# An attention block written out by hand: read-outs one per break, output products spread over more head pairs, row maxima turned in a score bank and sent by SyncE

## The chip, the cores and the metric

One core of a Trainium2 chip. The metric is the device time of one execution in microseconds; a kernel's time is the median of several executions. A profile is of one further execution, with its own time.

## The reference

A transformer block with adaptive layer norm: six modulation rows come from a condition vector, attention and a GELU feed-forward follow, each behind a normalization and in front of a gated residual. The attention is causal within four segments of 512 rows and reads a memory of the earlier segments:

```python
x = A_x                                   # 1 x 2048 x 512, 32 heads of 16
h = _layernorm(x) * (1 + ca) + sa
q, k, v = h @ wq, h @ wk, h @ wv          # split in 4 segments of L = 512
for s in range(4):
    logits = einsum("bhqd,bhkd->bhqk", qs, ks) * 16 ** -0.5 + mask
    a_dot = einsum("bhqk,bhkd->bhqd", softmax(logits), vs)
    pq = phi(qs)
    a_mem = (pq @ M) / (pq @ z + 1e-6)
    o = g * a_mem + (1 - g) * a_dot
    M, z = M + phi(ks).T @ vs, z + phi(ks).sum()
x = x + ga * (concat(o) @ wo)
h = _layernorm(x) * (1 + cb) + sb
x = x + gb * (gelu(h @ w1 + b1) @ w2 + b2)
```

## The kernel before, in words

The program is one stream per engine, in an order written out by hand. It has three parts: projections and memory (to about 195 us), attention (to about 620 us), and the feed-forward (to the end). The change lies in the second.

**Head pairs and quads.** The attention part runs over 64 head pairs P; two pairs make a quad Q (32 of them, 8 in each segment), two quads a unit U. The scores of a pair are made twice. `s_part` (L607) makes q times k in parts S0, S1, S2 for the pair P + 4, adds the causal mask by small bf16 products (L628), and VectorE takes the row maxima with `tensor_reduce` (L632). `st_part` (L681) makes k times q, already turned, in parts T0, T1, T2 for the pair P; the negated maxima ride along as three more rows of `qst` (51 rows in L672, 48 in L616), so that ScalarE's exponential (L691) can be taken at once. GpSimd zeroes what lies above the diagonal (L676).

**The maxima's way.** Once both pairs of a quad have their maxima, `m_rows` (L642, GpSimd) splits them into three bf16 terms; `m_put` (L649) turns them on TensorE with a product by an identity (L650) in the PSUM bank `mm`, ScalarE copies the result to `ms` (L124), and two DMAs (L654), issued by ScalarE, write it into rows 48 to 51 and 112 to 115 of the quad's `qst`.

**Read-out.** `pv_part` (L698) multiplies the exponentials of key block j (0 to 3) with V into the bank `pv`, for four heads side by side; block j covers columns 128j to 512. `pv_out` copies the bank to `ts` on ScalarE, and SyncE stores it (L717). Later `pv_in` loads it back with the denominators (L722, L724), `den` makes reciprocals and stores them (L744), `rb_in` loads them broadcast (L750), `mix` applies them, and `o_hi` and `o_lo` split the result.

**Output products.** For each segment but the last, and for each of its four row blocks b, four `wo_part` of three matmuls (L783) sum over the units into the bank `mm`, then `wo_out` adds the residual and SyncE stores it (L802). From these rows the second normalization takes its loads, statistics, applications and transposes (`ln2_*`; `ln2_turn`, L573, in bank `mm` for the first segment).

**The order.** `ORDER` writes out one head pair: `S0 T0 S1 c0 c1 c2 c3 c4 T1 S2 c5 c6 c7 c8 c9 T2`. Between the score parts are two breaks, c0 to c4 and c5 to c9. Everything else is placed by `ap(pos, ...)`: pair pos // 10, place pos % 10. The table `PRM` holds the places: `pv` and `pvout` relative to 20 Q, `mput` and `mrows` likewise, `wo` relative to a row block's start. All score parts of both kinds take the three PSUM score banks `att` in rotation (`bank("att")`), so a part can start only when the exponential or maximum of the part three before has left its bank. There is one bank `pv` and one `mm`; `own` checks that no two users of one overlap.

**SyncE** issues nearly all DMAs of this part in program order: the stores of the read-outs, the stacks `kst` and `qst` of a later quad (L174), the loads of `pv_in`, the reciprocals and the rows for the output products. An issue that waits for its data holds up all behind it.

## Time and profile before

| | us |
|---|---|
| median of 3 runs | 923.02 |
| lowest, highest | 919.65, 923.94 |
| profiled execution, its own time | 920.79 |
| span in its profile | 918.9 |
| first and last store of a read-out | 219.8, 606.1 |

Rows of the timeline show a start, a duration, engine, line, operation, tiles (out <- in), shape, how many instructions are merged, and in brackets the idle time before and what ended it. Rows of the windows view show the stretch, its length, then busy time (and instructions) of PE (TensorE matmuls), PEld (weight loads), DVE (VectorE), ACT (ScalarE) and POOL (GpSimd), then the granted TensorE clock as a share of full speed, the busy share of the DMA engines, and GB/s. Rows of the chain show a start, a length and what the chain passed through. Rows of the waits show the total, the number and the longest. ACTq and SPq are the sequencers of ScalarE and SyncE, where DMAs are issued.

### The profile page before, as it was taken

How to read it: one execution, taken by the hardware profiler on the slowest of the kernel's cores; microseconds unless marked ns; L12 is line 12 of the kernel's file. 1: busy time of each engine (PE TensorE's matmuls, PEld its weight loads, DVE VectorE, ACT ScalarE, POOL GpSimd, SP SyncE). 2: the span in 40 equal slices, each digit the busy share in tenths (PEclk: the TensorE clock that was granted, in tenths of full speed). 3: DMA queues.
4: the chain of work that ended last, by engine and by line, in shares of the span. 5: the costliest groups of instructions: out<-in, count | busy, mean ns of one | idle time of the engine just before them, and what ended most of it. 6: DMA issues, size and time to landing. Idle time of an engine off the chain costs nothing.

```text
span 918.9 us, 14721 instructions
## 1 busy us (share of the span) xinstructions
PE 849.3 (92%) x5289; PEld 577.5 (63%) x5289; DVE 537.2 (58%) x836; ACT 436.5 (48%) x688; POOL 299.5 (33%) x527
## 2 busy tenths in 40 slices
PE   9999999998888889888898889989999999999998
PEld 4877868664444445444444444457788888888887
DVE  7757674565555554555444555677666886553333
ACT  4454444235554554344344554637674533664221
POOL 2213434013564443434574453842310031330000
PEclk9999999997876997865797988989999999999999
DMA  8859464923445574654553465445756563545443
GB/s 324 282 207 348 168 223 151 355 69 95 130 126 121 133 176 114 156 138 112 137 146 105 129 174 156 141 125 197 234 191 235 179 222 111 170 151 179 154 139 114
DMA packets 97137, 156.53 MB, mean 170 GB/s; under 512 B 15396, under 2 KB 31652, under 8 KB 97064
## 3 DMA queue, kind: packets, MB, share of 16 engines
q1 hardware_dynamic: 94472, 153.24, 54.0%
q10 hardware_dynamic: 2592, 2.36, 0.8%
q8 instruction: 41, 0.67, 0.3%
q14 instruction: 32, 0.26, 0.1%
HBM read 93.95 MB, written 60.83 MB: 168 GB/s over the span
## 4 chain that ended last, share of the span: by engine, by line
PE 78%; ACT 6%; DMA 5%; ACTq 4%; DVE 3%; issue 3%; SPq 0%; POOL 0%; DVEq 0%
PE pv L706 11%; PE bx L1024 7%; PE att L672 6%; PE att L616 5%; PE mm L783 5%; PE bx L1289 5%; PE q L317 4%; PE by L1289 4%; PE bv L1289 4%; PE k L317 4%; ACTq L654 4%; ACT pt L691 4%; PE v L468 4%; PE bv L1024 3%; PE att L628 3%
## 5 line engine op out<-in xcount | busy, mean ns | idle before, releaser
L632 DVE TENSOR_REDUCE nm<-att 128x2 f32<-128x1024 f32 (+3 forms) x256 | 201.5, 821 | 184.5 <-PE att L628 160.9
L691 ACT ACTIVATE pt<-att 128x1024 f32<-128x1024 f32 (+1 forms) x192 | 166.2, 882 | 181.5 <-PE att L672 160.6
L676 POOL TENSOR_SCALAR_AFFINE_SELECT pt<-pt 128x256 f32<-128x256 f32 x256 | 103.4, 420 | 198.0 <-ACT pt L691 195.1
L616 PE MATMUL att<-kst,qst 48*128 48x512 f32 (+3 forms) x512 | 96.5, 405 | 52.3 <-ACT pt L691 47.6
L706 PE MATMUL pv<-pt,V 128*32 128x512 f32 (+2 forms) x992 | 108.9, 549 | 0.0
L672 PE MATMUL att<-qst,kst 51*128 51x512 f32 (+3 forms) x512 | 100.1, 421 | 4.8 <-DVE nm L632 4.0
L616 PEld LDWEIGHTS att<-kst,qst 48*128 48x128 f32 x512 | 55.8, 221 | 77.6 <-ACT pt L691 69.0
L672 PEld LDWEIGHTS att<-qst,kst 51*128 51x128 f32 x512 | 51.8, 213 | 56.3 <-DVE nm L632 29.8
L628 PE MATMUL att<-hmask,hid 64*128 64x128 bf16 (+1 forms) x768 | 74.9, 270 | 0.0
L820 POOL TENSOR_TENSOR wb<-wa 128x256 f32<-128x256 f32 x24 | 20.6, 858 | 153.3 <-DMA wa<-in_w 147.8
L706 PEld LDWEIGHTS pv<-pt,V 128*32 128x32 f32 x992 | 26.8, 125 | 37.5 <-issue 33.7
L133 DVE TENSOR_TENSOR gl<-s,gh 128x512 fp32r<-128x512 f32 x34 | 24.4, 718 | 40.9 <-ACT gh L130 40.8
L130 ACT ACTIVATE gh<-s 128x512 fp32r<-128x512 f32 x34 | 21.3, 629 | 46.5 <-PE spare L1289 18.6
L1029 ACT ACTIVATE s<-s,b1t 128x512 f32<-128x512 f32 x42 | 30.2, 720 | 17.9 <-DVE s L1033 17.8
L628 PEld LDWEIGHTS <-hid 64*128 64x128 bf16 x768 | 27.4, 108 | 17.4 <-issue 8.3
L1033 DVE TENSOR_TENSOR s<-bv,s 128x512 f32<-128x512 f32 x28 | 19.2, 686 | 24.4 <-PE bv L1024 19.2
L503 POOL TENSOR_SCALAR qp<-qp 128x512 f32<-128x512 f32 x12 | 18.5, 1539 | 40.7 <-ACT qp L498 40.7
L783 PE MATMUL mm<-woh,oh 128*128 128x512 f32 x52 | 26.9, 517 | 0.0
L317 PE MATMUL q<-Ahh,wqh 128*128 128x512 f32 x64 | 25.9, 404 | 0.0
L133 DVE TENSOR_TENSOR w1ml<-s,w1mh 128x512 fp32r<-128x512 f32 x18 | 13.0, 720 | 21.8 <-ACT w1mh L130 21.8
L317 PE MATMUL q<-Ahl,wqh 128*128 128x512 f32 x64 | 25.6, 400 | 0.0
L317 PE MATMUL k<-Ahh,wkh 128*128 128x512 f32 x64 | 25.4, 398 | 0.0
(355 smaller groups left out, 1942.3 us busy)
## 6 DMA issues: line engine op xcount, KB each, us to landing
GD<-s SPq DMA_DIRECT2D x56, 256.0 KB
s<-GD SPq DMA_DIRECT2D x52, 256.0 KB
kst<-KD SPq DMA_DIRECT2D x64, 192.0 KB
qst<-QD SPq DMA_DIRECT2D x64, 192.0 KB
QD<-q SPq DMA_DIRECT2D x16, 512.0 KB
KD<-k SPq DMA_DIRECT2D x16, 512.0 KB
TD<-ts SPq DMA_DIRECT2D x32, 256.0 KB
xt<-X2D SPq DMA_DIRECT2D x28, 256.0 KB
```

The source lines that it names most:

```text
L133: lo_eng.tensor_tensor(out=lo, in0=src, in1=hi.bitcast(F32), op=ALU.subtract)
L317: pe.matmul(ps, a[:, k, 128 * g:128 * g + 128], b[k], start=(k == 0 and i == 0), stop=(k == KB - 1 and i == 2))
L616: pe.matmul(ps[:, h, lo:lo + n], q_of(P, h, i), k_of(P, h, n), start=c == 0, stop=False, skip_group_check=True)
L628: pe.matmul(dst, hid[r, a], m, start=False, stop=a == 1, skip_group_check=True)
L632: v.tensor_reduce(out=nms[Q][:, 0:8:4, 4 * p + i], in_=ps[:, :, lo:lo + n], axis=AX.X, op=ALU.max, negate=True)
L672: pe.matmul(ps, k[r, P % 2, 128 * j:128 * j + 128], q[r, P % 2, 128 * j:512], start=True, stop=True, skip_group_check=True)
L676: pool.affine_select(out=t, in_=t, pattern=pattern, compare_op=ALU.is_ge, fill=0.0, base=0, channel_multiplier=-1)
L691: act.activation(pt, ps[:, :, :w], AF.Exp, scale=0.25)
L706: pe.matmul(ps[32 * c:32 * c + 32, lo:hi], V[4 * s + j][:, VW * hd:VW * hd + 32], pt[:, c // 2, lo - o:hi - o], start=start, stop=stop)
L783: pe.matmul(ps, a[:, 128 * b:128 * b + 128], w[:, g, :], start=(g == 0 and i == 0), stop=(g == 3 and i == 2))
L1024: pe.matmul(ps, a[:, i, k, :], b[k], start=start and k == 0 and c == 0, stop=k == 1 and c == 2, skip_group_check=not start)
L1289: pe.matmul(ps, a[:, c], w[:, lo:hi], start=(f == 0 and i == 0), stop=(last and i == 2))
```

## The change

Read-out parts: all quads now have key block 0 at c0 and block 1 at c5 of the even pair (the second pair after the quad's own first), block 2 at c0 and block 3 at c5 of the odd pair, one to each break. Before, block 0 stood in the even pair and the other three in the odd one, with two of them (three in the first segment) in one break.

Maxima: the turn is no longer placed by a table and no longer uses `mm`. It is one more product at the end of the score part S2 of an even pair, into columns 256 to 384 of that part's bank (for the last quad a bank of its own), with S2's own scores in columns 0 to 256. SyncE issues the two DMAs. In the first segment the turn stood at c1 of the odd pair before, in the others at c8 of the even pair; now it stands ahead of c5 of the even pair.

Output products: with `mm` free of the turns, the sixteen groups of the first two segments are placed singly, at most two to a pair, in the second half of the first break (c2) or in the second (c6), over ten pairs; those of the third over eight pairs, at c2 and c6. Before, each row block had two groups in one pair and two together at c0 of the next. The buffers of the split results go from five to six.

Second normalization: the first segment's statistics, applications and transposes move to later places; its transposes are done in two steps of two blocks in the score banks, in place of four single ones in `mm`.

```diff
- 'pv': [[[25, 0, 0, 512], [32, 1, 128, 512], [31, 2, 256, 512], [34, 3, 384, 512]],
- ...
+ 'pv': [[[20, 0, 0, 512], [25, 1, 128, 512], [30, 2, 256, 512], [35, 3, 384, 512]]] * 4,
- 'mput': [-9, -12, -12, -12],
- 'wo': [[2, 6, 10, 10], [2, 6, 10, 10], [2, 6, 10, 10]],
- 'woout': [10, 11, 11],
+ 'wo': [[2, 6, 16, 22, 26, 36, 42, 46, 56, 62, 66, 76, 82, 86, 102, 106]] * 2 + [[20 * b + i for b in range(4) for i in (2, 6, 12, 16)]],
- 'ht': [463, 481, 501, 521],
- 'ht1': 644,
- 'ln': [[312, 339, 374, 408], [531, 566, 603, 624]],
- 'lnl': [0, 4, 20, 24],
+ 'ht': [[465, 485], [644, 644]],
+ 'ln': [[345, 372, 412, 422], [531, 576, 611, 624]],
+ 'lnl': [0, 1, 20, 21],
- 'lnd': [[11, 10], [10, 2]],
+ 'lnd': [[11, 11], [10, 2]],
...
                     pe.matmul(dst, hid[r, a], m, start=False, stop=a == 1, skip_group_check=True)
+            if part == 2 and p == 0 and Q - 1 in nss:
+                m_put(Q - 1, ps[:, 0, 256:384], False)
             lo = 0
...
-        def m_put(Q):
-            pe.matmul(mm[:, :128], nss.pop(Q), identb, start=True, stop=True)
+        def m_put(Q, ps, start):
+            pe.matmul(ps, nss.pop(Q), identb, start=start, stop=True, skip_group_check=True)
             ms = sb.tile([64, 128], F32R, tag="ms", bufs=2, name=f"ms{Q}")
-            copy(PRM["mse"], ms, mm[:64, :128])
+            copy(PRM["mse"], ms, ps[:64])
             for h in range(2):
-                act.dma_start(qst[Q % NK][64 * h + 48:64 * h + 51].bitcast(F32), ms[32 * h:32 * h + 24].bitcast(F32))
+                sp.dma_start(qst[Q % NK][64 * h + 48:64 * h + 51].bitcast(F32), ms[32 * h:32 * h + 24].bitcast(F32))
...
-            oh = so.tile([128, 512], F32R, tag="oh", bufs=5, name=f"oh{U}")
+            oh = so.tile([128, 512], F32R, tag="oh", bufs=6, name=f"oh{U}")
...
-            ap(20 * Q + PRM["mput"][z], own, "mm", ("m", Q), m_put, (Q,), True)
...
+        def turn_pair(s, d):
+            t = bank("att")
+            for i in range(2):
+                ln2_turn(s, d + i, t[:, i])
...
+                    elif P + LEAD == NP and n == 2:
+                        m_put(NP // 2 - 1, bank("att")[:, 0, :128], True)
```

Three places show what that does to the order. TensorE, in the second break of an even pair in the second segment; `nm` are the maxima, `att` the score banks, L672 (now L668) is the score part T2, L616 (now L610) the next pair's S0. Before:

```order
L650 LDWEIGHTS nm_1910
L650 MATMUL mm<-identb,nm_1910 128x128
L672 MATMUL att_1919<-qst_1714,kst_1715 128x256 x2
L616 MATMUL att_1917<-kst_1939,qst_1938 128x512 x2
L628 LDWEIGHTS hid
```

Now:

```order
L646 LDWEIGHTS nm_1910
L646 MATMUL att_1918<-identb,nm_1910 128x128
L702 MATMUL pv_1920<-pt_1_3440,V_209 32x384
L702 MATMUL pv_1920<-pt_1_3511,V_209 32x384
L702 MATMUL pv_1920<-pt_1_3440,V_209 32x384
L702 MATMUL pv_1920<-pt_1_3511,V_209 32x384
L779 MATMUL mm<-woh,oh_3253 128x512
L779 MATMUL mm<-woh,ol_3255 128x512
L779 MATMUL mm<-wol,oh_3253 128x512
L668 MATMUL att_1919<-qst_1714,kst_1715 128x256 x2
```

The turn goes to the score bank that S2 has just filled, and a read-out part and a group of output products stand between it and T2, where before T2 followed the turn at once.

ScalarE, from the exponential of T1 to that of the next T0, in an even pair of the last segment; `ms` is the copy of the turned maxima, `pt` are exponentials. Before:

```order
L691 ACTIVATE pt_1_5336<-att_1917 128x1024
L124 ACTIVATE ms_5362<-mm 64x128
L654 DMA qst_1938<-ms_5362 3x8x128 x2
L691 ACTIVATE pt_2_5366<-att_1919 128x512
L691 ACTIVATE pt_0_5378<-att_1918 128x1024
```

Now:

```order
L687 ACTIVATE pt_1_5346<-att_1919 128x1024
L118 ACTIVATE ms_5361<-att_1917 64x128
L687 ACTIVATE pt_2_5376<-att_1918 128x512
L687 ACTIVATE pt_0_5388<-att_1917 128x1024
L118 ACTIVATE oh_5407<-opk_5092 128x512
```

The copy keeps its place; the two DMAs behind it are gone from this engine. In the built program VectorE's maximum of S2 in these pairs, which reads the same bank, waits for this copy.

SyncE, over one quad of the second segment; `TD` is the store of a read-out, `kst` and `qst` from `KD` and `QD` are the stacks, `RD` the reciprocals' store, `rbB` their broadcast load, `xb` and `X2D` the residual's load and the store of an output block. Before:

```order
L717 DMA TD_3530<-ts_3531 128x512
L174 DMA kst_2016<-KD_3_98 48x1024 x2
L174 DMA qst_2015<-QD_3_82 48x1024 x2
L802 DMA X2D_123<-xb_0_3337 128x512
L744 DMA RD_3584<-dn_3456 128x32
L792 DMA xb_2_3601<-in_x 128x512
L750 DMA rbB_3639<-RD_3584 128x1x512
L717 DMA TD_3530<-ts_3667 128x512
```

Now:

```order
L713 DMA TD_3530<-ts_3531 128x512
L168 DMA kst_2016<-KD_3_98 48x1024 x2
L168 DMA qst_2015<-QD_3_82 48x1024 x2
L740 DMA RD_3576<-dn_3465 128x32
L650 DMA qst_1721<-ms_3593 3x8x128 x2
L788 DMA xb_2_3605<-in_x 128x512
L746 DMA rbB_3638<-RD_3576 128x1x512
L798 DMA X2D_123<-xb_0_3346 128x512
L713 DMA TD_3530<-ts_3664 128x512
```

The two sends of the maxima stand behind the stack loads and the reciprocals' store, and ahead of the broadcast load.

## Prediction

> **What bounds the kernel now.** I read the page first, then the span in windows, then one steady stretch of the attention part engine by engine, then the waits.

> ```profile
> PE 849.3 (92%) x5289; PEld 577.5 (63%) x5289; DVE 537.2 (58%) x836; ACT 436.5 (48%) x688; POOL 299.5 (33%) x527
> PE 78%; ACT 6%; DMA 5%; ACTq 4%; DVE 3%; issue 3%; SPq 0%; POOL 0%; DVEq 0%
> ```

> The first line is busy time, the second the chain that ended last. TensorE (PE) carries it, but 4% is ACTq, ScalarE's sequencer busy issuing DMAs. All the change lies in the attention part, from about 195 to 620 us. The windows below give, for each stretch, the five engines' busy time, the granted TensorE clock, DMA share and GB/s.

> ```profile
> 195.00:620.00 425.00, 364.88 (x3024) 194.75 (x3022) 236.11 (x324) 209.36 (x296) 201.23 (x393) 0.83 0.50 132
> 302.47:312.61 10.14, 8.18 (x95) 4.25 (x92) 6.32 (x8) 6.23 (x10) 6.04 (x13) 1.00 0.52 135
> 392.68:406.28 13.60, 11.80 (x91) 5.72 (x89) 7.14 (x10) 5.84 (x9) 3.91 (x12) 0.63 0.46 126
> ```

> The second and third windows are one quad (two head pairs) each, from one store of the read-out to the next. The work on TensorE is the same but for a few records; one took 10.14 us at clock 1.00, the other 13.60 us at 0.63. So the part has two costs to look for: gaps within a quad, and a clock that is taken away. The gap at full clock, first on ScalarE, then on TensorE:

> ```profile
> 315.34 1.02 ACT L691 ACTIVATE pt<-att 128x1024 f32<-128x1024 f32 x1 [1.14 <-PE att L672]
> 316.26 0.26 ACT L124 ACTIVATE ms<-mm 64x128 fp32r<-64x128 f32 x1
> 316.55 1.50 ACTq L654 DMA_DIRECT2D qst<-ms  x2
> 318.15 1.51 ACT L691 ACTIVATE pt<-att 128x512 f32<-128x512 f32 x2 [1.63 <-PE att L672]
> ```

> ```profile
> 315.54 0.23 PE L650 MATMUL mm<-identb,nm 128*128 128x128 bf16 x1
> 315.70 0.38 PE L672 MATMUL att<-qst,kst 51*128 51x256 f32 x2
> 316.42 0.49 PE L616 MATMUL att<-kst,qst 48*128 48x512 f32 x2 [0.34 <-ACT pt L691]
> 316.85 0.47 PE L672 MATMUL att<-qst,kst 51*128 51x512 f32 x2
> 318.80 0.50 PE L616 MATMUL att<-kst,qst 48*128 48x384 f32 x4 [1.47 <-ACT pt L691]
> 319.47 1.28 PE L706 MATMUL pv<-pt,V 128*32 128x256 f32 x16
> 321.42 0.43 PE L706 MATMUL pv<-pt,V 128*32 128x128 f32 x8
> 322.31 0.57 PE L616 MATMUL att<-kst,qst 48*128 48x512 f32 x2 [0.15 <-ACT pt L691]
> ```

> ScalarE issues the two sends of the maxima from 316.55 to 318.05. The exponential of T2, whose scores TensorE finished near 316.1, starts only at 318.15, and the score product S1 that needs its bank waits 1.47 us. The trace calls the releaser ACT pt; behind it stands the sequencer. All the read-out that could have filled the hole (1.28 us, two parts together) stands just after it.

> The clock is next. These are stretches of 3.4 us, in the columns of the windows above.

> ```profile
> 303.80:307.20 3.40, 3.03 (x29) 1.33 (x22) 2.35 (x5) 1.48 (x3) 1.72 (x6) 1.00 0.85 229
> 310.60:314.00 3.40, 3.25 (x40) 2.02 (x44) 1.90 (x3) 2.83 (x4) 1.95 (x4) 1.00 0.16 61
> 395.90:399.30 3.40, 2.49 (x25) 1.32 (x21) 1.78 (x4) 1.18 (x2) 1.13 (x3) 0.99 0.74 139
> 399.40:402.80 3.40, 2.61 (x20) 1.27 (x24) 1.63 (x3) 1.51 (x2) 0.81 (x2) 0.50 0.22 79
> 498.30:501.70 3.40, 1.65 (x17) 0.76 (x15) 1.92 (x2) 1.77 (x4) 2.13 (x4) 1.00 0.32 96
> 501.80:505.20 3.40, 3.27 (x24) 1.46 (x28) 1.29 (x2) 1.51 (x3) 2.08 (x3) 0.51 0.55 162
> ```

> The clock is 0.50 or 1.00 in such stretches. A full-clock stretch with TensorE busy 1.65 or 2.49 us is followed by one at half; after 3.03 and 3.25 none does (the quad from 302.47 to 312.61 stayed at 1.00). The stretches that fall are those with the maxima's stall and with no read-out or output product in them. I take it that the activity of one stretch sets the clock of the next. [...]

> **The change part by part.** The sum is made against the profiled execution, 920.79 us (span 918.9 us), 2.2 us below the median of 923.02.

> *Maxima sent by SyncE.* Sixty-four issues leave ScalarE.

> ```profile
> L654 ACTq DMA_DIRECT2D qst<-ms x64: 728/729/1354, 196.4 to 586.9; - x64
> ```

> That is 0.73 us each, 1.5 us in a quad, and 1.47 us of it stands on TensorE. What is late next is S1 by the exponential itself: T2's scores end at 316.1, an exponential of half the 1.51 us for two brings that to 316.9, and S1 could follow T0 at 317.3 without a wait. I count 29 of 32 quads (not the first, nor the last two, behind which no score products are left): 29 x 1.47 = 42.6 us; bounds 0 and 32 x 1.47 = 47.

> *Maxima turned earlier.* In the first segment the turn stood one break into the odd pair, and the next quad waited for its rows:

> ```profile
> ACT pt L691 <- DMA qst<-ms: 9.7, 6, 1.6
> ```

> It moves to S2 of the even pair, more than half a pair earlier. Six waits, 9.7 us as ScalarE saw them; TensorE had work for part of that. I take 6 us, bounds 4 and 9.7. In the other segments it only moves ahead of the second break.

> *The turn in a score bank.* In the built program VectorE's maximum of S2 in these pairs now waits for ScalarE's copy of the turned maxima, which reads the same bank ahead of it; and that copy waits for T1's exponential. By the ScalarE rows the copy is done at 316.5, and this is when S2's maximum runs today:

> ```profile
> 315.72 0.69 DVE L632 TENSOR_REDUCE nm<-att 128x2 f32<-128x512 f32 x1
> 317.16 1.23 DVE L632 TENSOR_REDUCE nm<-att 128x2 f32<-128x1024 f32 x1 [0.75 <-PE att L628]
> ```

> So it would end near 317.2 instead of 316.4. T0, which takes that bank, starts at 316.85 today, but now the read-out part of 384 columns stands ahead of T2, which by the 1.28 us for 256 and 384 together is 1.28 x 384/640 = 0.77 us, so T0 comes near 317.6: covered. Queued behind it on VectorE is S0's maximum at 317.16, which slips by a tenth. Zero; 0.4 us x 30 = 12 if the cover is gone.

> *Read-outs one per break, products spread.* No matmul is added or dropped. At full clock the read-outs cost what they cost; what they bring is that they fill holes and that the clock may stay. An output product group alone costs more than one of a pair, since its first weights load is not hidden:

> ```profile
> 332.88 0.89 PE mm L783 x3
> 335.54 1.57 PE mm L783 x6
> ```

> These are rows of the chain: a group of three alone, and two groups together. Four groups of 0.89 in place of two and a pair of 1.57: 3.56 - 3.35 = 0.21 us, x 12 = +2.5 us.

> The clock: a mean of 0.83 over 425 us is 2 x 0.17 x 425 = 144 us at half. Its price, from the two quads: 13.60 - 10.14 = 3.46 us for 2 x 0.37 x 13.60 = 10.1 us at half, 0.34 us each; 144 x 0.34 = 49 us in all. With the stall gone and a read-out part in every break, the stretches that fell would be fuller; where output products run, nearly every break holds some work. What stays thin is the odd pair of a quad without products, whose two parts are the short ones (0.43 us for the last). I give a third of the price to those: 33 us back, bounds 0 and 49.

> *First normalizations moved, turns in score banks.* The same statistics, applications and transposes; but four turned blocks now take a turn of the score banks in two pieces, and two activations must empty each before it comes round. A stall of about one exponential (1.02 us) for each piece: +2 us, bounds 0 and 4. The loads and POOL's applications have slack of pairs.

> *SyncE's queue.* Each quad's two sends now stand behind that quad's stack loads and every second time behind the store of the reciprocals.

> ```profile
> 312.61 0.34 SPq L717 DMA_DIRECT2D TD<-ts  x1
> 313.52 0.86 SPq L174 DMA_DIRECT2D kst<-KD  x2
> 314.44 0.88 SPq L174 DMA_DIRECT2D qst<-QD  x2
> 316.15 0.34 SPq L744 DMA_DIRECT2D RD<-dn  x1
> 322.53 0.60 SPq L750 DMA_DIRECT2D rbB<-RD  x1
> 323.23 0.40 SPq L717 DMA_DIRECT2D TD<-ts  x1
> ```

> ```profile
> 248.01 5.61 DMA qst<-QD
> 273.59 3.53 DMA qst<-ms
> ```

> SyncE is free at 316.5, when the copy is ready; two issues at the pace of its others (0.86 for two) and 3.53 us to land give 320.9. The T0 that reads the rows follows S0 (322.31) by half a microsecond, 322.8 today and 321.3 with the hole gone: 0.4 us of slack. The stack loads are as tight: issued by 315.3, landed after up to 5.61 us, at 320.9, and needed by S0 at 322.3 today, 320.8 then. A third of a microsecond of wait in each of some 15 quads without products: +5 us; bounds 0 and 1 us x 16. In quads with products TensorE has more to do in the meantime.

> Sum: 42.6 + 6 + 33 - 2.5 - 2 - 5 = 72 us, so 920.8 - 72.1 = 849 us.

> **The rivals.**

> *The clock comes back whole.* Then 16 us more, 833 us, and with every other term at its better bound 920.8 - 47 - 9.7 - 49 + 2.5 = 818 us. For it: the quad at 302.47 held its clock even with the stall. Against: the thin odd pair. Chance 0.13.

> *The clock does not move.* If what fell was not the thin stretch, or if a shorter quad only brings the thin stretches closer, the 33 us stay lost: 849 + 33 = 882 us, up to 886 with the bank and queue terms half as large again. [...] Chance 0.15.

> *SyncE's row becomes the bound.* With quads of 8.7 us (10.14 - 1.47) the store of a read-out waits behind the broadcast load (322.53), which waits for the reciprocals' store; the stack loads behind it are late in every second quad.

> ```profile
> SPq L717 <- ACT ts L124: 157.2, 29, 11.3
> SPq L750 <- DMA RD<-dn: 39.1, 15, 4.6
> ```

> 39.1 us over 15 is 2.6 us each time, today hidden in the 5.4 us that SyncE waits for each read-out copy. If a third of it shows, 0.8 us x 32 = 26 us: 875 us. [...] No row here shows a send behind loads. Chance 0.14.

> *Slower: the maxima starve T0.* The same queue, but the sends themselves held up: if SyncE reaches them later than the 0.4 us of slack worked out above, every quad waits and TensorE, idle again, loses its clock as now. The gain without the clock is 42.6 + 6 - 9.5 = 39 us, so it turns at 39/32 = 1.2 us beyond the slack, and at 3 us beyond (SyncE's wait of up to 4.6 us falling ahead of the sends) it is 920.8 - 39 + 96 = 978 us. In the order of instructions the wait stands behind the sends, which speaks against it. Chance 0.05.

> *It does not act:* the 1.47 us turn out to be the exponential's own lateness and another wait takes their place, 918 to 925 us. The exponential's start 0.1 us after the second issue speaks against it. Chance 0.03.

> **How the numbers follow.** The forecast, 835 to 866 us (the clock term half as large again or half gone), has 0.50. The range 820 to 886 takes in the whole clock at one end and the unmoved clock with the queue terms at the other, and leaves out the starved case and a queue much worse than priced. About 0.5% (4.6 us) is what a measurement of this kernel can tell from no change: faster by more 0.50 + 0.13 + 0.15 + 0.14 = 0.92, within it 0.03, slower 0.05.

> **What would show it.** Right: no DMA issues on ScalarE in the attention part; the wait of S1 for ACT pt falls from 1.47 us to under 0.3; stores of the read-outs some 8.7 us apart in quads without products and 11.4 with three groups of them; the mean clock from 195 us to the last store above 0.92; that part some 70 us shorter, the rest of the span as before. Wrong: S0 or T0 waiting for kst, qst or ms DMAs in most quads; 3.4-us stretches at half clock as often as now; VectorE's S2 maximum waiting and T0 behind it.

## The result, and the profile after

The changed kernel takes 841.78 us (median of 4 runs, 839.78 to 846.23) against 921.34 us before (4 runs, 918.22 to 923.94): ratio 0.9144, 95% interval 0.9095 to 0.9194. The forecast was 849, with 820 to 886 as its range. The profile below is of an execution of 846.23 us, the longest of the four. Ratios here and below compare, for each kernel, the runs within 1.5% of its fastest, so that a ratio can differ from the quotient of two medians.

Page of the changed kernel, busy time and chain:

```profile
PE 805.5 (96%) x5289; PEld 551.6 (65%) x5289; DVE 535.6 (64%) x836; ACT 437.5 (52%) x688; POOL 297.3 (35%) x527
PE 70%; DMA 10%; POOL 6%; ACT 5%; DVE 4%; issue 3%; SPq 2%; ACTq 0%; DVEq 0%; POOLq 0%
```

TensorE does the same 5289 instructions in 44 us less, and ACTq has left the chain. All that follows is read from one stretch, from the first store of a read-out to the last: before first, then after (window, its length, then busy us of PE, PEld, DVE, ACT, POOL; granted clock, DMA share, GB/s).

```profile
219.83:606.09 386.26, 332.20 (x2800) 173.19 (x2797) 206.88 (x289) 193.30 (x272) 186.57 (x370) 0.82 0.52 137
```

```profile
217.19:529.76 312.57, 290.71 (x2801) 148.87 (x2798) 206.24 (x289) 194.20 (x272) 185.25 (x370) 0.97 0.64 169
```

The stretch is 73.7 us shorter; the rest of the span moved by 2 us. The row splits the gain in two. Length less PE's busy time is TensorE's idle time: 54.1 us before, 21.9 after, so 32.2 us. The other 41.5 us is busy time: the same matmuls in 290.7 us instead of 332.2, at a clock of 0.97 instead of 0.82, which makes 19 us at half (2 x 0.03 x 312.6) instead of 139. The clock has two digits, so each such figure is good to some 4 us.

Now quads of the changed kernel: without products, with them, and the three longest.

```profile
273.20:281.40 8.20, 7.96 (x92) 4.06 (x90) 6.49 (x9) 5.79 (x9) 4.09 (x13) 1.00 0.62 166
318.50:329.00 10.50, 10.40 (x100) 5.30 (x100) 6.23 (x8) 6.56 (x9) 7.22 (x14) 1.00 0.65 162
233.70:246.60 12.90, 8.99 (x102) 4.72 (x99) 6.60 (x10) 6.90 (x10) 7.03 (x15) 0.99 0.50 124
379.40:391.90 12.50, 9.41 (x91) 4.90 (x91) 7.75 (x12) 5.90 (x10) 6.56 (x12) 0.91 0.65 174
414.50:429.50 15.00, 13.26 (x100) 6.87 (x101) 6.68 (x9) 6.44 (x10) 9.45 (x16) 0.77 0.50 132
```

A steady quad takes 8.2 us, with TensorE idle for 0.24 of it, or 10.5 with three groups of products. The forecast said 8.7 and 11.4. What is left to gain stands in the last three rows. Waits, in the form "who <- whom: us in total, times, longest":

```profile
DVE nm L628 <- ACT ms L118: 39.9, 31, 2.4
PE att L610 <- ACT pt L687: 6.3, 14, 3.0
PE att L610 <- DMA qst<-QD: 3.2, 3, 1.8
PE att L668 <- DVE nm L628: 1.0, 2, 0.6
```

S1's wait for the exponential is 6.3 us where it was 46.3 over 51. VectorE's wait for the turned maxima has come in its place, 31 times, but TensorE waits for VectorE only twice.

### The profile page after: what moved, and what is told of

The parts are those of the page before. It is cut to its first block, busy times and chain, and to the rows that moved or that the text cites. A ratio compares the mean times of both kernels' runs of the same rounds, so it can differ in the third digit from the quotient of the medians.

```text
span 843.3 us, 14733 instructions
## 1 busy us (share of the span) xinstructions
PE 805.5 (96%) x5289; PEld 551.6 (65%) x5289; DVE 535.6 (64%) x836; ACT 437.5 (52%) x688; POOL 297.3 (35%) x527
## 3 DMA queue, kind: packets, MB, share of 16 engines
q10 hardware_dynamic: 864, 1.57, 0.6%
## 4 chain that ended last, share of the span: by engine, by line
PE 70%; DMA 10%; POOL 6%; ACT 5%; DVE 4%; issue 3%; SPq 2%; ACTq 0%; DVEq 0%; POOLq 0%
PE bx L1024 7%; PE bx L1289 5%; PE pv L702 5%; PE q L311 5%; PE by L1289 5%; PE bv L1289 5%; PE att L668 4%; PE k L311 4%; PE att L610 4%; PE v L462 4%; PE mm L779 4%; PE bv L1024 3%; ACT pt L687 3%; DMA qst<-QD 3%; PE spare L1289 2%
## 5 line engine op out<-in xcount | busy, mean ns | idle before, releaser
L628 DVE TENSOR_REDUCE nm<-att 128x2 f32<-128x1024 f32 (+3 forms) x256 | 200.0, 821 | 107.9 <-PE att L622 54.6
L687 ACT ACTIVATE pt<-att 128x1024 f32<-128x1024 f32 (+1 forms) x192 | 168.6, 882 | 109.6 <-PE att L668 90.0
L672 POOL TENSOR_SCALAR_AFFINE_SELECT pt<-pt 128x256 f32<-128x256 f32 x256 | 101.5, 413 | 125.8 <-ACT pt L687 125.2
L610 PE MATMUL att<-kst,qst 48*128 48x512 f32 (+3 forms) x512 | 85.8, 355 | 14.1 <-ACT pt L687 6.3
L702 PE MATMUL pv<-pt,V 128*32 128x512 f32 (+1 forms) x992 | 96.5, 462 | 0.0
L668 PE MATMUL att<-qst,kst 51*128 51x512 f32 (+3 forms) x512 | 92.1, 391 | 2.4 <-DVE nm L628 1.0
L668 PEld LDWEIGHTS att<-qst,kst 51*128 51x128 f32 x512 | 46.3, 192 | 70.9 <-DVE nm L628 50.0
L610 PEld LDWEIGHTS att<-kst,qst 48*128 48x128 f32 x512 | 49.4, 193 | 33.1 <-ACT pt L687 22.5
L622 PE MATMUL att<-hmask,hid 64*128 64x128 bf16 (+1 forms) x768 | 68.9, 248 | 0.0
L124 ACT ACTIVATE gh<-s 128x512 fp32r<-128x512 f32 x34 | 21.3, 628 | 46.9 <-PE spare L1289 17.5
L622 PEld LDWEIGHTS <-hid 64*128 64x128 bf16 x768 | 25.4, 98 | 14.6 <-issue 8.1
L702 PEld LDWEIGHTS pv<-pt,V 128*32 128x32 f32 x992 | 19.8, 109 | 19.6 <-issue 13.9
```

Of the source, the lines that this page charges most:

```text
L610: pe.matmul(ps[:, h, lo:lo + n], q_of(P, h, i), k_of(P, h, n), start=c == 0, stop=False, skip_group_check=True)
L622: pe.matmul(dst, hid[r, a], m, start=False, stop=a == 1, skip_group_check=True)
L628: v.tensor_reduce(out=nms[Q][:, 0:8:4, 4 * p + i], in_=ps[:, :, lo:lo + n], axis=AX.X, op=ALU.max, negate=True)
L668: pe.matmul(ps, k[r, P % 2, 128 * j:128 * j + 128], q[r, P % 2, 128 * j:512], start=True, stop=True, skip_group_check=True)
L672: pool.affine_select(out=t, in_=t, pattern=pattern, compare_op=ALU.is_ge, fill=0.0, base=0, channel_multiplier=-1)
L687: act.activation(pt, ps[:, :, :w], AF.Exp, scale=0.25)
```

## The experiments

Twelve kernels ran in three groups of four, each group on a chip of its own and beside the kernel before. Since before alone ranged from 903 to 930 us there, causes are read more from the stretch, in one profile of each kernel, than from the times. Its row for each kernel stands under its verdict, and "idle" and "at half" are worked out from it as above.

**Sends alone.** Before, with one word changed in m_put:

```
-                act.dma_start(qst[Q % NK][64 * h + 48:...
+                sp.dma_start(qst[Q % NK][64 * h + 48:...
```

> The kernel before with only the sending engine changed: SyncE issues the two sends, all else in its old place. Theory: the 1.47 us wait of S1 goes, 43 us, and with it a part of the half-clock time, since the stretches that fell held the stall: 850 to 878 us, ratio 0.92 to 0.955; the turn of the first segment still waits for its rows. Rival one (the gain needs the filled breaks, as another wait takes the stall's place): over 905 us. Rival two (stall goes, clock does not move): 876 to 880 us.

Measured: 877.40 us (870.77 to 886.70), ratio 0.9565 (0.9452 to 0.9678). Stretch, and the wait that is new:

```profile
216.49:561.49 345.00, 301.92 (x2801) 165.37 (x2798) 204.96 (x289) 193.99 (x272) 185.54 (x370) 0.90 0.56 153
PE att L616 <- ACT pt L691: 14.3, 28, 1.3
PE att L672 <- DMA qst<-ms: 22.0, 9, 4.6
```

At half 69 us, idle 43.1. The stall fell from 46.3 to 14.3 us and half of the lost clock came back though no read-out was moved. (By its time alone the second rival, an unmoved clock, would fit as well.) But nine times T0 starves for its maxima: the mechanism of the slower rival, at up to 4.6 us. ScalarE's copy and then SyncE's queue in one of these quads:

```profile
311.03 0.26 ACT L124 ACTIVATE ms<-mm 64x128 fp32r<-64x128 f32 x1
```

```profile
313.35 0.63 SPq L722 DMA_DIRECT2D dn<-TD  x1
314.02 0.59 SPq L724 DMA_DIRECT2D opk<-TD  x1
314.65 0.46 SPq L731 DMA_DIRECT2D amB<-AMD  x1
315.15 0.50 SPq L792 DMA_DIRECT2D xb<-in_x  x1
315.75 1.59 SPq L654 DMA_DIRECT2D qst<-ms  x2
```

The maxima are ready at 311.3, but at the old place of the turn the sends stand behind the loads that read TD back. Those wait for the store to land (2.2 us here), and the sends leave at 315.75. In all nine quads such loads of TD stand ahead of the sends. So it is the place in SyncE's order, not the time of an issue, that decides.

**The turn's new place.** The changed kernel with both tables as before, `'pv'` and `'wo': [[20 * b + i for b in range(4) for i in (2, 6, 10, 10)]] * 3`; first with SyncE's sends, then with ScalarE's. Both also keep the later normalizations, their transposes in score banks and the sixth buffer, so they are not the new place quite alone.

> The changed kernel with both tables put back: read-outs and output products where they stood before; sends on SyncE, maxima turned at their new place in a score bank. Theory (stall and clock are one cause; without the stall few stretches are thin): 842 to 860 us, half-clock time under 70 us, S1's wait gone. Rival (the spread is what holds the clock and hides the sends): about the 877 us of the sends alone. Against the kernel with the sends alone it isolates the new place of the turn: theory says that the waits for late rows (22 us there) go.

> As the kernel with both tables put back, but with ScalarE issuing the sends: the new place of the turn alone. Theory: the issue starts one read-out part earlier than before, so S1's wait falls from 1.5 to about 1.1 us, and some clock returns: 885 to 905 us. Rival (the place does nothing by itself, and the 44 us that place and tables brought together come from the tables): 915 to 922 us.

Measured: with SyncE 864.48 us (858.27 to 866.11), ratio 0.9447 (0.9348 to 0.9545); with ScalarE 910.79 us (902.07 to 923.94), ratio 0.9972 (0.9913 to 1.0031). Stretches, the first with its waits:

```profile
217.54:547.92 330.38, 299.49 (x2800) 158.98 (x2797) 203.65 (x289) 192.78 (x272) 186.47 (x370) 0.92 0.59 160
PE att L613 <- ACT pt L690: 13.2, 29, 0.8
PE att L671 <- DVE nm L631: 8.7, 27, 0.6
237.90:251.70 13.80, 11.45 (x95) 5.79 (x92) 6.58 (x9) 6.47 (x10) 6.38 (x14) 0.63 0.39 117
```

```profile
219.34:595.96 376.62, 325.73 (x2800) 169.66 (x2797) 205.92 (x289) 192.74 (x272) 187.74 (x370) 0.85 0.53 140
```

The place alone gives no time that can be told from none (the forecast of 885 to 905 for it fell). With SyncE's sends the nine waits for the maxima's rows are gone, and the kernel falls from 877 to 864 (15 us of the stretch), a little above what was expected. The two ran on different chips and the intervals of their ratios just overlap, so the waits that are gone show the cause better than the 13 us show its size. What stays is the clock in the first segment (the 13.80-us quad at 0.63) and, with the old read-out table, 27 waits for VectorE. Of these, 15 stand ahead of T0, 3.7 us or 0.25 each: none stand there in before or with the sends alone, so this is the cost of the turn in a score bank where no read-out part covers it. The others, ahead of T1 and T2, were there before.

**ScalarE's sends, all else as changed.**

> The changed kernel with only the sending engine undone: ScalarE issues the two sends of the maxima again, at their new place. Theory (the issues stall TensorE, and the stall takes the clock down): 1.5 us of issue stand again ahead of an exponential in 29 quads, up to 29 x 1.47 = 43 us, less where a read-out part now stands behind the issue and fills some of it (0.77 us at most); with some clock lost besides, 865 to 890 us, ratio to before 0.94 to 0.97. Rival (what gained was the spread work, that holds the clock; the queue of the sends is of no account): 838 to 848 us, ratio 0.91 to 0.92.

Measured: 875.49 us (868.14 to 877.38), ratio 0.9553 (0.9456 to 0.9650).

```profile
219.30:560.08 340.78, 306.68 (x2800) 153.17 (x2797) 209.63 (x289) 192.77 (x272) 186.75 (x370) 0.92 0.59 155
PE att L610 <- ACT pt L687: 22.6, 32, 1.0
```

Idle 34.1, at half 55 us. The issues cost 34 us by the medians and 28 of the stretch, a time in the range that the theory gave: 12 idle, 16 busy at the lower clock. The wait is 0.7 us each instead of 1.5, since the issue now starts ahead of a read-out part.

**The tables.** The read-out table alone in the kernel before; the changed kernel with the old read-out table; and with the old product table.

> The kernel before with only the read-out table changed: one part in each break of the next quad; sends still on ScalarE, output products still in pairs. Theory (clock set by how much TensorE does in a stretch of 3.4 us): the stall of 1.47 us stays, but more stretches hold a read-out, so part of the 49 us of clock comes back: 885 to 910 us, ratio 0.96 to 0.99, mean clock of the attention part above 0.88. Rival (the clock falls with the stall itself, or by an idle gap, and the place of the read-outs does not matter): 917 to 925 us, clock 0.83 as before.

> The changed kernel with only the read-out table put back (read-outs bunched at four old places, output products spread). Theory: at full clock they cost the same; in plain quads the break before T2 of the odd pair stays empty and some stretches fall: 842 to 855 us. Rival (one read-out per break is what keeps the exponentials covered): over 860 us.

> The changed kernel with the output products back on eight head pairs of a segment, two groups together at the last break, as before. Theory: single groups cost 2.5 us more at full clock, but thin odd pairs without them lose some clock, and the last two groups come two thirds of a pair earlier: 840 to 850 us. Rival (the spread of the products carries a large part of the clock's return): over 855 us.

Measured: 916.89 us (908.46 to 921.90), ratio 1.0027 (0.9973 to 1.0081); 863.80 us (856.67 to 865.36), ratio 0.9447 (0.9360 to 0.9533); 845.60 us (838.14 to 852.48), ratio 0.9214 (0.9091 to 0.9338). Their stretches, in this order:

```profile
218.94:605.05 386.11, 336.01 (x2801) 169.99 (x2798) 208.58 (x289) 194.90 (x272) 186.96 (x370) 0.82 0.51 137
```

```profile
216.79:545.33 328.54, 298.50 (x2801) 156.64 (x2798) 206.36 (x289) 194.00 (x272) 186.14 (x370) 0.91 0.59 161
```

```profile
213.18:534.54 321.36, 304.12 (x2800) 155.51 (x2797) 205.09 (x289) 194.22 (x272) 185.90 (x370) 0.92 0.61 164
315.60:327.00 11.40, 11.27 (x105) 6.10 (x105) 6.92 (x9) 6.45 (x10) 6.92 (x13) 1.00 0.61 156
```

With the stall in place the read-out table brings nothing, time or clock, as the rival said: my reason for it, that a part in every break fills the thin stretches, fails as it stood. With the stall gone it brings 864 - 842 = 22 us by the medians and 16 us of the stretch, with 40 us less at half and 8 less idle. That is more than I expected (842 to 855 without it); the time lies where the rival put it, over 860. Of the half-clock time with the old read-out table, 44 of 58 us lie in the first segment, which has no output products to fill its breaks. The product table is worth 4 us by the medians, which the scatter of these runs does not separate from nothing. Four groups in a quad cost 11.4 - 8.2 = 3.2 us, 0.8 each; three groups at single places cost 10.5 - 8.2 = 2.3, 0.8 each. The extra weights load that I had charged does not show.

**Is it the clock, and what sets it?** Before, with work added where TensorE stalls; `ones` is a constant tile, and nothing reads the product.

```
+                if 0 < P < NP and tok == ("S0" if P < 16 else "S1") and P % 2 == (P >= 16) and not busy.get("mm"):
+                    for _ in range(6):
+                        pe.matmul(mm.rearrange("p (c n) -> p c n", c=4), ones, ones.unsqueeze(1).to_broadcast([128, 4, 128]), start=True, stop=True)
```

> The kernel before with nothing moved and work added: in 31 quads six matmuls of a constant tile (128x128 on 512 columns, bf16, written to the idle bank mm and never read) stand where TensorE waits for the exponential behind ScalarE's two issues. The stall of 1.1 to 1.6 us stays as time, but TensorE is busy in it. Theory (the clock of a 3.4-us stretch is set by how much of the array worked in the one before): the half-clock time of the attention part falls from 136 us to under 45, and at 0.34 us each the kernel gains about 31 us although it does more: 885 to 900 us. Rival one (clock set by something else, such as only long idle gaps or heat): half-clock time as before, 919 to 930 us. Rival two (the stall was hiding other waits, which come later with the added work): slower than before.

Measured: 884.63 us (883.12 to 885.91), ratio 0.9689 (0.9616 to 0.9762). The stall of one quad, TensorE and ScalarE's queue, and the stretch:

```profile
304.86 1.51 ACTq L656 DMA_DIRECT2D qst<-ms  x2
```

```profile
305.58 1.47 PE L969 MATMUL mm<-ones 128*128 128x512 bf16 x6
307.12 0.50 PE L618 MATMUL att<-kst,qst 48*128 48x384 f32 x4
216.08:564.58 348.50, 325.65 (x2975) 166.42 (x2974) 206.45 (x289) 193.02 (x272) 186.48 (x370) 0.98 0.56 152
```

The kernel does more work, keeps every send on ScalarE, and is 31 us faster than before: at half 14 us instead of 139. The runs also lie within 0.3% of each other, where before scatters by 3%. Nothing else in the attention part was touched, so the clock follows what TensorE does in such a hole.

The size can be put closer. In the stretch of before the clock stays at 0.5 for 3.41, 6.83, 10.24, 13.65 or 20.48 us at a time, in that of the changed kernel for 3.41 or 6.83: whole multiples of 3.41 us. I split the stretch of each of the fourteen kernels into steps of this length and gave each a fill, an estimate: the time that its matmuls stream, weighted by the rows and columns that the profile gives for them, as a share of 128x128 (48*128 for a score product, 128*32 for a read-out). 512 columns at full clock count 0.22 us, from the row of six above: (1.47 - 0.38)/5, with 0.38 us for one matmul by itself. For the read-outs I took twice that, an assumption; it fits that a part of 512 columns, two matmuls for each of four heads side by side, takes 1.06 us. Of 1145 steps at full clock, those filled under 0.35 were followed by half clock 89 times in 101; from 0.35 to 0.40, 27 in 61; from 0.40 to 0.45, 2 in 71; above, never in 912. From half, with the step measured at that clock, 49 of 50 under 0.65 stayed, and 40 of 41 above 0.80 came back; of the more than 100 between, about half stayed. Streaming time without the weight separates worse: with the best boundary some 60 of the full-clock steps stand on the wrong side, with it some 24. That holds only with the factor of two: with the read-outs counted once it is some 66 with the weight and 58 without.

**The turn in a score bank.** One letter, `'mse': 'v'`: VectorE copies the maxima itself.

> The changed kernel with the turned maxima copied by VectorE instead of ScalarE, so that VectorE's maximum of S2 no longer waits for ScalarE's copy (39.9 us of waits over 31 quads in the changed kernel). Theory (this wait is covered by the read-out part ahead of T2, so the turn in a score bank costs nothing): 839 to 845 us, no change. Rival (the wait starves T0 and costs 0.4 us in 30 quads): 828 to 834 us.

Measured: 837.04 us (834.26 to 838.82), ratio 0.9179 (0.9125 to 0.9233).

```profile
272.60:280.90 8.30, 8.11 (x96) 4.12 (x93) 6.61 (x10) 5.72 (x8) 4.01 (x13) 1.00 0.58 161
318.00:328.50 10.50, 10.40 (x100) 5.29 (x102) 6.43 (x10) 6.41 (x8) 7.23 (x14) 1.00 0.68 180
```

The time lies between the two expectations; the quads decide. With the wait gone they take 8.3 and 10.5 us, as with it (8.2 and 10.5): covered, as predicted. What this run has less of is half clock (clock 0.99 in the stretch, against 0.97); whether the copy brings that, or chance, is open.

**The three long quads.** In the changed kernel SyncE, ahead of the 12.9-us quad's stack loads:

```profile
233.68 0.35 SPq L713 DMA_DIRECT2D TD<-ts  x1
237.22 0.36 SPq L864 DMA_DIRECT2D wor<-in_wo  x1
237.66 0.85 SPq L168 DMA_DIRECT2D kst<-KD  x2
```

It waits 3.2 us at a load of output weights, whose buffer GpSimd has not freed, with the stack loads behind it. In the 15.0-us quad the maxima's rows stand behind normalizations on GpSimd. The two waits:

```profile
SPq L864 <- POOL nm L642: 3.3, 1, 3.3
PE att L646 <- POOL nm L642: 4.0, 5, 1.5
```

Three kernels, each the changed one with edits: the first edit, the second, and all three:

```
-                ap(ln[3] + ld[1] * b, ln2_apply, i, b, (pool, v)[i])
+                ap(ln[3] + ld[1] * b, ln2_apply, i, b, v)
```

```
- 'wl': [17, 66, 80, 81],
+ 'wl': [30, 66, 80, 81],
```

```
- 'lnl': [0, 1, 20, 21],
+ 'lnl': [0, 8, 20, 28],
```

> The changed kernel with the first segment's four normalizations applied by VectorE instead of GpSimd. In the changed kernel they take 2.07 us each on GpSimd and the maxima's rows of one quad stand behind them: TensorE's turn waits 1.48 us and that quad takes 15.0 us, half of it at half clock. On VectorE the same operation takes 0.58 us. Theory: that quad falls to about 11 us, 836 to 840 us against 842. Rival (VectorE is the tighter engine: it delays the score maxima instead): 842 to 846 us.

> The changed kernel with the loads of the output weights 13 breaks later, so that the fourth is issued after its buffer has been freed. In the changed kernel SyncE waits there for GpSimd, the stack loads behind it are issued 3 us late, and the quad takes 12.9 us where its neighbours take 8.25, followed by one with half clock. Theory (one queue in order: what waits at its head delays all behind it): 3 to 5 us gained, 837 to 840 us. Rival (the loads were late by the transfers, not by the issue): 841 to 844 us.

> The two edits together (normalizations on VectorE, weight loads later), and the first loads of the normalizations spread over four pairs instead of two. In the changed kernel two of these loads of 256 KB stand ahead of stack loads that landed after 11.35 us, with S0 waiting 3.0 us. Theory: the 15.0, 12.9 and 12.5 us quads all fall towards their neighbours and the half clock behind them goes: 829 to 836 us, the fastest of all. Rival (each mended wait only makes the next one late): 838 to 844 us.

Measured on one chip: 839.77 us (835.98 to 841.59), ratio 0.9203 (0.9141 to 0.9265); 837.81 us (834.09 to 840.21), ratio 0.9188 (0.9132 to 0.9243); 833.56 us (830.37 to 837.58), ratio 0.9147 (0.9089 to 0.9206). The long quads of the third, and its stretch; then the one quad of the first and the one of the second that their edits are aimed at:

```profile
233.40:242.80 9.40, 8.16 (x95) 4.10 (x93) 6.50 (x9) 6.49 (x10) 6.37 (x14) 1.00 0.72 206
378.30:386.80 8.50, 8.43 (x88) 4.26 (x86) 7.37 (x12) 5.85 (x8) 6.31 (x12) 1.00 0.82 204
408.00:418.70 10.70, 10.40 (x100) 5.31 (x100) 7.41 (x11) 6.32 (x9) 5.23 (x12) 1.00 0.66 160
216.91:517.94 301.03, 285.97 (x2801) 145.94 (x2798) 209.61 (x293) 194.17 (x272) 178.20 (x366) 0.99 0.66 175
```

```profile
412.20:422.90 10.70, 10.40 (x100) 5.32 (x100) 7.41 (x11) 6.31 (x9) 5.23 (x12) 1.00 0.58 158
233.40:242.80 9.40, 8.16 (x95) 4.10 (x93) 6.49 (x9) 6.49 (x10) 6.35 (x14) 1.00 0.78 204
```

All three fell: 12.9 to 9.4, 12.5 to 8.5, 15.0 to 10.7 us; the stretch is 11.5 us shorter than the changed kernel's. But not all of that is the edits' work. The kernel with VectorE's copy, of the same group, has none of them, and these are the same quads there:

```profile
234.40:245.70 11.30, 9.06 (x98) 4.73 (x98) 6.63 (x10) 6.70 (x10) 7.09 (x16) 0.97 0.46 140
378.00:387.50 9.50, 9.07 (x94) 4.73 (x92) 7.87 (x13) 5.74 (x8) 6.28 (x12) 1.00 0.77 217
408.10:420.30 12.20, 10.42 (x100) 5.26 (x100) 6.77 (x10) 6.16 (x8) 9.31 (x16) 1.00 0.51 135
```

Against these the edits are worth 1 to 2 us of a quad; the rest of the fall came without them, some of it as half clock. That whole stretch takes 302.8 us, 1.8 more than with the three edits. The three edits together make the fastest kernel measured, though its runs overlap with those of the kernels beside it: 833.56 us against 837.04 with VectorE's copy and none of the edits. The changed kernel did not run in that group, and the ratios of different groups, 0.9147 and 0.9144, rest on reference runs that scatter by 3%. By the times it would be 841.78 - 833.56 = 8 us, about 1%; by the ratios none. The quads speak for a small gain, but its size is not settled.

## Why the prediction was right, and where its steps were off

**Sends: right in cause, 42.6 us split otherwise.** Alone they gave 42 us, and taking them back cost 34. But of the 41 us by which sending alone shortens the stretch, 30 are clock, since 22 us of starving came back as idle time. And the idle time of the whole change fell by 32.2 us, where my idle terms (42.6 + 6 - 2 - 5) made 41.6.

**The clock: mis-sized, 33 us for some 41.5.** The step that failed is "what stays thin is the odd pair of a quad without products": those quads ran at 1.00 in 8.2 us, so the third that I left to them came back too. The price of 0.34 us for each us at half holds: 41.5/(139 - 19) = 0.35. It is a mean, as the order of the parts moves the busy time too: with both old tables and with the old product table alone, 53 and 51 us at half, TensorE is busy for 299.5 and 304.1 us. Its cause was half wrong as well. I gave it to the spread, and the read-out table without the sends returned none of it.

**The turn's place: 6 us, measured some 13 (877 to 864).** I priced only the first segment's late rows. Its worth is that the sends leave ahead of the read-back in SyncE's queue. The slower rival, which I gave 0.05, is real: with SyncE's sends and without this part of the change T0 starves in nine quads, in the changed kernel in none.

**The turn in a score bank: zero, as said, and for the reason given.** Without the cover T0 waits 15 times for 0.25 us, 3.7 us in all, where 0.4 us x 30 = 12 stood as the bound.

**Products: +2.5 us, not seen. Transposes in score banks: +2, seen.** TensorE's wait for their activations rose from 2.1 to 3.7 us.

```profile
PE att L569 <- ACT hr L571: 3.7, 4, 1.1
```

**SyncE's queue: 5 us, right in size, not in place.** I saw a third of a microsecond in each of 15 quads; it came as 3.9 - 0.2 and 3.1 - 0.2 us of idle time in two quads, where a weight load and loads of 256 KB stood ahead of the stack loads.

**The rivals.** The clock that stays did not come about: of 139 us at half, 19 are left. In the stretch of before no idle time of TensorE was longer than 1.85 us, and filling those of the stall took the half-clock time from 139 to 14 us. So idle times this short cost the clock here, where the step around them held too little. SyncE's row, the rival at 875 us, did not become the bound either: steady quads run at 8.2 us, with 0.24 us of idle time in all. Nor did the sends come too late behind the stack loads: in the stretch of the changed kernel TensorE waits for none of them.

The whole comes to 79.6 us by the medians (74.6 by the profiled runs) against 72. That the sum came so near is luck in part: idle time was taken 9 us too high, and clock 8.5 us too low.

## What to carry to other kernels

A DMA issue belongs on a queue whose engine nobody waits for (moving the sends alone gave 42 us), and there ahead of every entry that waits itself: that place was worth some 13 us here. When TensorE's clock falls, count idle and busy time apart, since a short hole was paid twice here, as idle time and as clock (11 and 30 us of the 41 by which the sends alone shorten the stretch); work put into the hole, even useless work, shows which of the two one pays for. Changes that bring nothing alone (the read-out table, the turn's place) can bring 16 and 15 us of a stretch once the first stall is gone, so test the parts both ways: alone, and taken back.

## What the runs showed of the hardware

Adding 186 matmuls, some 40 us of TensorE work (186 x 0.22), made the kernel 31 us faster.

Beside each other on one chip, before ranged from 904 to 930 us in 13 runs, while the filled kernel kept to 883 to 886 in 4. No run shows where this scatter comes from.
